# A GFNet mixing block followed by a SiLU feed-forward network: how the start of the kernel and its first 24 steps are arranged

## The chip, the core and the metric

The kernel runs on one core of a Trainium2 chip, in one launch. The metric is the device time of a run in microseconds. Five engines work beside each other: TensorE (PE; its weight loads are PEld), VectorE (DVE), ScalarE (ACT), GpSimd (POOL) and SyncE (SP). Each works through its own queue in the order in which the program issued its instructions[...].

## The reference

The input is `x` of 8 x 3008 x 256. It is filtered in the frequency domain along its second axis, and the result goes through a feed-forward network (FFN) row by row:

```python
X = np.fft.rfft(x, axis=1)
Y = X * (filt_r + 1j * filt_i)[None]
y = np.fft.irfft(Y, n=3008, axis=1).reshape(24064, 256)
h = y @ w_in                        # 256 x 2048
g = h * (1.0 / (1.0 + np.exp(-h)))
out = g @ w_out                     # 2048 x 256
```

The two weight matrices arrive in 64-bit floating point; the kernel rounds them to 32 bits on the chip.

## The kernel before

**The spectral part.** The Fourier transform of 3008 points is done as matrix products of 94 and 64 points, one batch at a time, in six groups `g`. `forward(g)` (L438) makes the second forward product on TensorE, `multiply(g, k)` (L454) multiplies it by the two filter parts on VectorE out of PSUM, `add(g, k)` combines the four products to a complex number, `inverse` goes back, `rows` evicts and writes to a DRAM tensor `d2`, `load_t4` reads `d2` back in another order, and `stage3` (L549) makes `y`, in two halves of each batch.

**The ramp.** Batch 0 cannot hide behind an FFN, since there is none yet. From L1028 on the program writes its order out by hand: `stage1_first` and 16 transposes, then per group `forward`, `multiply`, `inverse_first` (L495), `rows_first` (L515). For groups 0 and 1 GpSimd adds the products (`by_gpsimd`, L1010). For groups 2 to 5 nobody adds them: `inverse_first` runs twice as many matmuls and lets PSUM add. `load_t4` reads `d2` in three portions of rows (0 to 24, 24 to 32, 32 to 48), eight transfers each, some of them on the ACT queue. The four `stage3` calls that follow make the first half of `y`; then FFN step 0 can start.

**The FFN.** The tokens are cut in 48 pairs of blocks of n tokens (256, 256 and 240 in each half of a batch). Each pair needs 8 steps, one for each index `jp` of 256 hidden columns, 384 steps in all. A pair of blocks is multiplied by Strassen's method with 7 products instead of 8, so `tokens(pair)` (L709) first makes 4 differences on VectorE. A step runs two generators against each other: `hidden(step)` (L719) makes 7 products and the SiLU, and `project(step - 1)` (L778) makes 7 products of the step before, which add up over the 8 steps in four PSUM banks `acc` 0 to 3. `drain(pair, i)` (L803) copies a bank out after the eighth step; GpSimd then makes 7 sums, and `output` (L840) transposes and stores.

**Rounds.** Each step has 8 rounds (0 to 7). In a round each generator goes one product further, then `until` emits all pieces that are due. The hidden products of rounds 0 to 7 are: A11 into bank `px`; A12 into `pyz[:, 1]`, then VectorE makes g0 from it; S2 into `px`; S1 into `pyz[:, 0]`; S3 into `px`, then VectorE makes g2; nothing; A22 into `px`; S4 into `pyz[:, 0]`, then VectorE makes g1 from it. `px` and `pyz` have one buffer each. P0 to P6 below are the products of `project` in their order. `put(step, rnd, piece)` (L593) sets when a piece of spectral work or of weight work is emitted; a piece of a round comes after that round's products on every queue.

**Opened steps.** For 20 steps in the list `opened` (two for batch 1, three for each later batch) the program emits P0, P1 and some spectral products ahead of round 0. So `project` is two ahead and is held back in two rounds (L1154):

```python
held = work[1:] if step in opened and rnd in (0, 2) else []
work = [w for w in work if w in held or next(w, work) is not work]
```

**The weights.** 16 blocks `j` of weights are loaded raw (`load_weights`, L880), split into exponent and mantissa (`split_weights`, L907: two VectorE instructions, L920 and L923, and two on ACT), rounded (`round_weights`, L933: three on VectorE, L936, L938, L942), multiplied together into `w_t` (`place_weights`, L945: two, L951), and for each two blocks combined (`combine_weights`, L961: four). Blocks 0 to 8 are done before the FFN. Blocks 9 to 15 are done in steps 0 to 6:

```python
for j in range(9, NJ):
    put(j - 9, 1, lambda j=j: (split(j), rounded(j)))
    put(j - 9, 5, placed, j)
```

Their combining is put at round 5 mostly. Steps 0 to 7 also hold the `stage1` of batch 1, four matmuls in round 3 (L333, tile `pa`).

Of the kernel before, what the change touches and what calls it, by code (L numbers as in the profile page):

```python
# [167 lines left out]
def kernel(  # L168
# [98 lines left out]
    def spectral(b):  # L267
# [12 lines left out]
        def load_first():  # L280
# [10 lines left out]
            return view  # L291
# [162 lines left out]
        def multiply(g, k):  # L454
            if b == 0 and g == NG - 1:

                room = raws["first"].bitcast(FP32).rearrange("p (k i r c) -> p k i r c", k=2, i=2, r=2)
                z, pt = room[:, k, 0], room[:, k, 1]
            else:
                z = zpool.tile([128, 2, C], FP32, name=f"z_{b}_{g}_{k}", tag="z")  # L460
            if b == 0 and g == NG - 1:
                pass
            elif b == 0 and k == 1:
                pt = abcpool.tile([128, 3, C], FP32, name=f"p_{b}_{g}_{k}", tag="abc")[:, 0:2]
            else:
                pt = ppool.tile([128, 2, C], FP32, name=f"p_{b}_{g}_{k}", tag="p")
# [6 lines left out]
        def add(g, k):  # L473
            z, pt = prods[g][k]
            eng = nc.vector if b > 0 else nc.gpsimd
# [19 lines left out]
        def inverse_first(g):  # L495
# [3 lines left out]
            pairs = prods.pop(g)  # L499
            halves[g] = ps  # L500
            for h in range(2):
                table = e_t[:, g] if h == 0 else minus[g // 4][:, g % 4]
                terms = [(table[:, :, 0], 0, 0), (table[:, :, 1], 0, 1)]
                if g not in by_gpsimd:
                    terms += [(table[:, :, 1], 1, 0), (neg[h][:, g], 1, 1)]
                for t, (lhs, which, ri) in enumerate(terms):
                    for i in range(2):
                        rows = slice(64 * i, 64 * i + 64)
                        for k in range(2):

                            nc.tensor.matmul(out=ps[i][64 * k:64 * k + 64, h, :], lhsT=lhs[rows, k],
                                             rhs=pairs[k][which][rows, ri, :], start=(h == 0 and t == 0),
                                             stop=(t == len(terms) - 1), skip_group_check=True)

        def rows_first(g):  # L515
            for i, pool, tag in ((0, qpool, "q"), (1, opool, "o")):
                qt = pool.tile([128, 2, C], FP32, name=f"q_{b}_{g}_{i}", tag=tag)
                nc.scalar.copy(out=qt, in_=halves[g][i])
                a0 = 8 * g + 4 * i
                queue = nc.gpsimd if g == NG - 2 else nc.scalar  # L520
                queue.dma_start(out=d2[a0:a0 + 4].rearrange("a n h c -> (a n) h c"), in_=qt)
# [17 lines left out]
        def load_t4(g, first=0, last=2 * NS):  # L539
            if first == 0 and b == 0 and g in (2, 3):  # L540
                t4s[g] = tpool.tile([128, 4, C], FP32, name=f"t4_{b}_{g}", tag="t")
            elif first == 0:
                t4s[g] = t4pool.tile([128, 4, C], FP32, name=f"t4_{b}_{g}", tag="t4")
            for h in range(2):
                queue = nc.scalar if first == 32 and h == 1 else nc.sync
                queue.dma_start(out=t4s[g][64 * h + first:64 * h + last],
                                in_=d2[first:last, 4 * g:4 * g + 4, h, :])
# [30 lines left out]
        def evict_y(g, h):  # L578
# [7 lines left out]
                    load_t2=load_t2, forward=forward, multiply=multiply, add=add, inverse=inverse, inverse_first=inverse_first, rows_first=rows_first, even=even, rows=rows, load_t4=load_t4, stage3=stage3)  # L586
# [114 lines left out]

    def combine(eng, out, in0, in1, op):
        eng.tensor_tensor(out=out, in0=in0, in1=in1, op=op)  # L703
# [5 lines left out]
    def tokens(pair):  # L709

        n, yt = pairs[pair][3], channels(pair)
        t = typool.tile([128, 4, CH], FP32, name=f"ty_{pair}", tag="ty")
# [4 lines left out]
        ty[pair] = t  # L717

    def hidden(step):  # L719

        pair, jp = divmod(step, NJP)
        n, yt, t = pairs[pair][3], channels(pair), ty[pair]
# [55 lines left out]
    def project(step):  # L778

        pair, jp = divmod(step, NJP)  # L780
        n, g = pairs[pair][3], g_t.pop(step)
        if jp == 0:
            acc[pair] = {}
        last = jp == NJP - 1

        order = PROJECT
        if jp == 0 and step in joined:
            order = PROJECT[0:2] + PROJECT[3:5] + PROJECT[2:3] + PROJECT[5:]
        elif jp == 0:
            order = PROJECT[2:3] + PROJECT[0:2] + PROJECT[3:]  # L790
        for c, k, i, h in order:
            if i not in acc[pair]:
                acc[pair][i] = accps.tile([128, 2, 256], FP32, name=f"acc_{pair}_{i}", tag=f"a{i}")

            nc.tensor.matmul(out=acc[pair][i][:, h, 0:n], lhsT=w_t[:, jp, c, 1], rhs=g[:, k, 0:n],  # L795
                             start=(jp == 0 and h == 0), stop=last, skip_group_check=True)
            if last and (h == 1 or i == 3):
                drain(pair, i)
# [4 lines left out]
    def drain(pair, i):  # L803
        n = pairs[pair][3]

        if i == 0:
            results[pair] = spool.tile([128, 8, CH], FP32, name=f"s_{pair}", tag="s")
            if n < CH:
                gp.memset(results[pair][:, :, n:CH], 0.0)
        s = results[pair]  # L810
        if pair == len(pairs) - 1:
            return drain_last(pair, i, n, s, acc[pair])
        copy = v.tensor_copy if i % 2 else nc.scalar.copy
        if i < 3:
            copy(out=s[:, 2 * i:2 * i + 2, 0:n], in_=acc[pair][i][:, :, 0:n])  # L815
            return
        copy(out=s[:, 6, 0:n], in_=acc.pop(pair)[3][:, 0, 0:n])
        for o, a, b in ((2, 0, 2), (5, 0, 5), (3, 5, 3), (6, 3, 6), (0, 5, 1), (4, 0, 4), (1, 3, 1)):
            combine(gp, s[:, o, 0:n], s[:, a, 0:n], s[:, b, 0:n], ALU.add)

    def drain_last(pair, i, n, s, sums):

        def add(o, a, b):
            combine(v, s[:, o, 0:n], s[:, a, 0:n], b, ALU.add)
        if i == 0:
            nc.scalar.copy(out=s[:, 0:2, 0:n], in_=sums[0][:, :, 0:n])
# [361 lines left out]
```

## Time and profile before

| what | value |
|---|---|
| time, median of 3 runs | 2586.41 us (2585.56 to 2587.24) |
| the profiled execution, its time / its span | 2588.03 us / 2586.3 us |
| mean granted TensorE clock | 0.995 |
| busy: PE, PEld, DVE, ACT, POOL | 99%, 85%, 65%, 43%, 16% |
| PE busy in the first 100 us | 85.67 us |
| first matmul of FFN step 0 | 82.36 us |

The page gives shares over the whole span. The ramp is 3% of it, so anything that happens there has to be read from the timeline and the chain of waits for the first 100 us. From 82 us on, the profile can be read step by step: each step begins with a matmul into `px` from `y`. A plain step lasts 6.04 us with n = 256 and 5.67 us with n = 240; one with `stage1` in it mostly 7.84 to 7.97 us.

### The profile page before, as it was taken

The page shows a single profiled execution, that of the slowest core. Times are in us where ns is not written, and L with a number is a line of the kernel's source. Part 1 is how long each engine was busy: PE and PEld are TensorE (multiplying, and loading weights), DVE is VectorE, ACT ScalarE, POOL GpSimd, SP SyncE. Part 2 cuts the span into 40 slices and gives each one's busy share as a digit, 9 for nine tenths or more (in the row PEclk, how much of TensorE's full clock was granted, in tenths as well). Part 3 has the DMA queues.
Part 4 walks back from the last instruction along what each step waited for, and adds up shares of the span by engine and source line. Part 5 has one row for each costly group of instructions (what it writes and reads, how often), then busy time and mean ns, then how long its engine had stood idle before and what let it go on. Part 6 is the DMA issues. An engine that isn't in the chain of part 4 may idle for free.

```text
span 2586.3 us, 48366 instructions
## 1 busy us (share of the span) xinstructions
PE 2560.6 (99%) x18972; PEld 2198.1 (85%) x18972; DVE 1681.0 (65%) x3569; ACT 1113.9 (43%) x3014; POOL 424.9 (16%) x672
## 2 busy tenths in 40 slices
PE   8999999999999999999999999999999999999998
PEld 6688888888888888888888888888888888888987
DVE  7766666666666766666666666666666676555554
ACT  3544444444444444444444444444444444444443
POOL 2211211121112111211122111211121112101101
PEclk9899999999999999999999999999999999999999
DMA  8431232212222222231223222331232211210000
GB/s 276 142 90 45 68 83 67 60 53 82 63 63 64 71 65 58 70 78 59 68 51 89 58 66 58 79 76 52 64 74 67 73 45 27 65 20 16 9 17 17
DMA packets 200077, 171.08 MB, mean 66 GB/s; under 512 B 122116, under 2 KB 174196, under 8 KB 199060
## 3 DMA queue, kind: packets, MB, share of 16 engines
q1 hardware_dynamic: 178520, 117.04, 19.0%
q0 software_dynamic: 16928, 44.65, 5.4%
q10 hardware_dynamic: 4400, 6.29, 0.8%
q8 instruction: 149, 2.44, 0.4%
q14 instruction: 80, 0.66, 0.1%
HBM read 96.05 MB, written 81.26 MB: 69 GB/s over the span
## 4 chain that ended last, share of the span: by engine, by line
PE 95%; DVE 2%; DMA 1%; ACT 1%; issue 0%; ACTq 0%; SPq 0%; DVEq 0%
PE acc L795 43%; PE px L732 25%; PE pyz L732 19%; PE pd L560 3%; PE pb L446 2%; PE pc L489 2%; PE pf L416 1%; DMA w_t<-in_x_dram 0%; DVE g L703 0%; PE pa L342 0%; DMA filt<-in_filt_r_dram 0%; DMA d_t<-d_tbl 0%; PE pa L333 0%; DMA raw<-in_moe_w_out_dram 0%; ACT t L349 0%
## 5 line engine op out<-in xcount | busy, mean ns | idle before, releaser
L795 PE MATMUL acc<-g,w_t 128*128 128x256 f32 (+1 forms) x5376 | 1508.7, 375 | 0.4 <-DVE g L703 0.4
L795 PEld LDWEIGHTS acc<-g,w_t 128*128 128x128 f32 x5376 | 1021.3, 190 | 115.6 <-DVE g L703 0.8
L703 DVE TENSOR_TENSOR g<-pyz,abc 128x256 f32<-128x256 f32 (+1 forms) x1152 | 479.7, 416 | 614.9 <-ACT abc L753 360.1
L703 DVE TENSOR_TENSOR g<-g 128x256 f32<-128x256 f32 (+3 forms) x1152 | 599.3, 520 | 196.9 <-ACT g L736 183.7
L732 PE MATMUL px<-ty,w_t 128*128 128x256 f32 (+1 forms) x2304 | 678.1, 376 | 0.5 <-ACT abc L753 0.5
L736 ACT ACTIVATE g<-g 128x256 f32<-128x256 f32 (+1 forms) x1152 | 472.9, 410 | 250.1 <-DVE g L703 250.1
L703 POOL TENSOR_TENSOR s<-s 128x256 f32<-128x256 f32 (+1 forms) x329 | 255.1, 793 | 1412.7 <-DVE s L815 1307.6
L732 PEld LDWEIGHTS px<-ty,w_t 128*128 128x128 f32 x2304 | 432.3, 190 | 64.5 <-issue 8.2
L732 PE MATMUL pyz<-y,w_t 128*128 128x256 f32 (+1 forms) x1536 | 454.2, 377 | 0.0
L732 PEld LDWEIGHTS pyz<-y,w_t 128*128 128x128 f32 x1536 | 283.4, 189 | 48.3 <-DVE g L703 8.6
L747 ACT COPY abc<-px 128x256 f32<-128x256 f32 (+1 forms) x384 | 141.5, 368 | 364.6 <-PE px L732 364.6
L753 ACT COPY abc<-px 128x256 f32<-128x256 f32 (+1 forms) x384 | 141.9, 370 | 336.1 <-PE px L732 335.3
L736 ACT ACTIVATE g<-px 128x256 f32<-128x256 f32 (+1 forms) x384 | 146.1, 381 | 297.3 <-PE px L732 297.2
L732 PE MATMUL px<-y,w_t 128*128 128x256 f32 (+1 forms) x768 | 232.2, 384 | 2.0 <-ACT y L246 1.0
L732 PE MATMUL pyz<-ty,w_t 128*128 128x256 f32 (+1 forms) x768 | 225.7, 376 | 0.2 <-DVE g L703 0.2
L732 PEld LDWEIGHTS px<-y,w_t 128*128 128x128 f32 x768 | 140.3, 189 | 34.9 <-DVE y L582 5.8
L732 PEld LDWEIGHTS pyz<-ty,w_t 128*128 128x128 f32 x768 | 144.5, 190 | 18.8 <-DVE g L703 1.0
L740 ACT COPY abc<-px 128x256 f32<-128x256 f32 (+1 forms) x384 | 135.8, 354 | 45.0 <-PE px L732 45.0
L560 PEld LDWEIGHTS pd<-wi_t,t 48*64 48x64 f32 x4096 | 67.2, 138 | 30.9 <-ACT g L736 16.4
L560 PE MATMUL pd<-wi_t,t 48*64 48x47 f32 x4096 | 73.5, 236 | 5.7 <-issue 3.5
L428 POOL DMA_DIRECT2D d<-tf x144 | 71.7, 505 | 31.3 <-DVE tf L424 27.3
L815 ACT COPY s<-acc 128x512 f32<-128x512 f32 (+1 forms) x94 | 54.3, 578 | 47.5 <-PE acc L795 47.4
(118 smaller groups left out, 1312.7 us busy)
## 6 DMA issues: line engine op xcount, KB each, us to landing
t<-d SPq DMA_DIRECT2D x120, 192.0 KB
d<-q POOLq DMA_DIRECT2D x86, 256.0 KB, 2.6
t<-d SPq DMA_DIRECT2D x84, 256.0 KB
out_dram<-o SPq DMA_DIRECT2D x636, 32.0 KB
d<-tf POOLq DMA_DIRECT2D x144, 96.0 KB, 3.5
xr<-in_x_dram SPq DMA_DIRECT2D x6, 1472.0 KB
x_all<-in_x_dram SPq DMA_DIRECT2D x72, 96.0 KB
x_all<-xr SPq DMA_DIRECT2D x72, 96.0 KB
```

What stands on the lines that cost most here:

```text
L428: nc.gpsimd.dma_start(out=d1[k // 2, :, k % 2, n0:n0 + 4], in_=us["tf"][32 * k:32 * k + NS].rearrange("p q n c -> p (q n) c"))
L446: nc.tensor.matmul(out=ps[k][32 * j:32 * j + 32, ri, :], lhsT=d_t[rows, 4 * g + at, ri, :], rhs=t2[rows, at, :], start=True, stop=True)
L489: nc.tensor.matmul(out=ps[j][64 * k:64 * k + 64, a, :], lhsT=e_t[rows, g + a, k, ri, :], rhs=zs[k][rows, ri, :], start=(a == 0 and ri == 0 ...
L560: nc.tensor.matmul(out=ps[h][c0:c0 + 64, cb, i, :], lhsT=t4s[g][rows, i, 128 * cb + c0:128 * cb + c0 + 64], rhs=wi_t[rows, :], start=True, ...
L703: eng.tensor_tensor(out=out, in0=in0, in1=in1, op=op)
L732: nc.tensor.matmul(out=out, lhsT=w_t[:, jp, c, 0], rhs=rhs, start=start, stop=True, skip_group_check=True)
L736: nc.scalar.activation(out=g[:, k, 0:n], in_=g[:, k, 0:n] if src is None else src, func=AFT.Silu)
L740: nc.scalar.copy(out=sums[:, 0, 0:n], in_=xo)
L747: nc.scalar.copy(out=sums[:, 1, 0:n], in_=xo)
L753: nc.scalar.copy(out=sums[:, 2, 0:n], in_=xo)
L795: nc.tensor.matmul(out=acc[pair][i][:, h, 0:n], lhsT=w_t[:, jp, c, 1], rhs=g[:, k, 0:n], start=(jp == 0 and h == 0), stop=last, skip_group ...
L815: copy(out=s[:, 2 * i:2 * i + 2, 0:n], in_=acc[pair][i][:, :, 0:n])
```

## The change

**Ramp.** `load_t4` for the first half of `y` is replaced by `load_t4_first`: one area of 16 KB per partition, read by six transfers on SP (rows 0 to 16, 16 to 32, 32 to 48, two each). GpSimd adds the products of all groups, with VectorE taking the second of groups 4 and 5; `inverse_first` has 32 matmul instructions for every group. The first four `forward` calls are issued together. The last eviction of `rows_first` goes to VectorE. ACT's first filter loads wait for the last piece of `x` and no longer for the second. Blocks 0 to 3 of the weights are done before the FFN, instead of 0 to 8.

**FFN.** The first three pairs are cut in two runs each: `jp` 0-1 of pair 0, 0-3 of pairs 1 and 2, then the rest of each. The first run is copied out of PSUM, the second is added to it by VectorE. So the later weights are needed later, blocks 4 to 15 are done in steps 0 to 10 and 12, and their VectorE work is spread over more rounds. `tokens` runs six times for these pairs. The rounds in which an opened step holds `project` back are 1 and 2 instead of 0 and 2.

```diff
+        def load_t4_first(first, last):
+            for g in range(4):
+                t4s[g] = us["t4"][:, 4 * g:4 * g + 4]
+            for h in range(2):
+                nc.sync.dma_start(out=us["t4"][64 * h + first:64 * h + last], in_=d2[first:last, 0:16, h, :])
...
         def add(g, k):
             z, pt = prods[g][k]
-            eng = nc.vector if b > 0 else nc.gpsimd
+            eng = nc.vector if b > 0 or (g > 3 and k == 1) else nc.gpsimd
...
-                terms = [(table[:, :, 0], 0, 0), (table[:, :, 1], 0, 1)]
-                if g not in by_gpsimd:
-                    terms += [(table[:, :, 1], 1, 0), (neg[h][:, g], 1, 1)]
-                for t, (lhs, which, ri) in enumerate(terms):
+                for ri in range(2):
...
+                copy = nc.vector.tensor_copy if (g, i) == (NG - 1, 1) else nc.scalar.copy
+                copy(out=qt, in_=halves[g][i])
...
+    runs = [(0, 0, 2), (1, 0, 4), (2, 0, 4), (0, 2, 8), (1, 4, 8), (2, 4, 8)]
+    runs += [(pair, 0, NJP) for pair in range(3, len(pairs))]
...
+        if begin > 0:
+            combine(v, dst, dst, src, ALU.add)
+        else:
+            copy = v.tensor_copy if i % 2 else nc.scalar.copy
+            copy(out=dst, in_=src)
...
+    def round_weights(j, k):
...
+        if k == 0:
...
             v.tensor_scalar(out=e, in0=hi, scalar1=20, scalar2=0x7ff,
                             op0=ALU.logical_shift_right, op1=ALU.bitwise_and)
+            v.tensor_scalar(out=m, in0=hi, scalar1=0xfffff, scalar2=None, op0=ALU.bitwise_and)
+        elif k == 1:
             nc.scalar.activation(out=ef, in_=e, func=AFT.Relu, bias=bias_t[:, 0:1])
...
+        elif k == 2:
             v.scalar_tensor_tensor(out=mf, in0=lo, scalar=2.0 ** -52, in1=mf, op0=ALU.mult, op1=ALU.add)
-            if j not in (0, 2, 4, 6):
+            if not by_scalar:
                 v.tensor_scalar(out=e, in0=ef, scalar1=255.0, scalar2=float(1 << 23),
                                 op0=ALU.min, op1=ALU.mult)
-        for j in js[::-1]:
-            lo, hi, e, m, ef, mf = raws[j]
+        else:
             v.scalar_tensor_tensor(out=e, in0=hi, scalar=0x80000000, in1=e,
                                    op0=ALU.bitwise_and, op1=ALU.bitwise_or)
...
+    for g in range(4):
         part["forward"](g)
     for g in range(NG):
         for k in range(2):
             part["multiply"](g, k)
+            part["add"](g, k)
+        if g == 3:
+            part["forward"](5)
+        if g > 0:
+            inverse(g - 1)
+        if g == 1:
             part["forward"](4)
+    part["load_t4_first"](0, 16)
+    part["load_t4_first"](16, 32)
+    inverse(NG - 1)
+    part["load_t4_first"](32, 48)
+    second["load_x"](0)
+    weights(4, 5)
+    second["load_x"](1)
     combine_weights(0)
+    for k in range(4):
+        for j in (2, 3):
+            round_weights(j, k)
+    placed(2, 3)
+    combine_weights(1, eng=gp)
+    weights(6, 7)
+    idle(26)
     for g in range(4):
         part["stage3"](g)
-    weights(11, 12, 13)
+    weights(8, 9)
...
-    for j in range(9, NJ):
-        put(j - 9, 1, lambda j=j: (split(j), rounded(j)))
-        put(j - 9, 5, placed, j)
+    for j in range(4, NJ):
+        at = j - 4 if j < 15 else 12
+        for k, rnd in enumerate((1, 2, 4, 5)):
+            put(at, rnd, round_weights, j, k)
+        put(at, 6, placed, j)
         if j % 2:
...
+            for k, rnd in ((0, 3), (1, 5)):
+                put(at + 1, rnd, combine_weights, j // 2, k)
...
+    joined.update((2, 6, 10, 20))
...
+    begun = ((-2, 1), (0, 5), (4, 5), (8, 5), (14, 5), (18, 5))
+    early_stores = (((22, 1), (22, 5)), ((23, 1), (23, 5)), ((26, 1), (26, 4)))
...
-            held = work[1:] if step in opened and rnd in (0, 2) else []
+            held = work[1:] if step in opened and rnd in (1, 2) else []
```

## The prediction

> **What bounds the kernel now.** I read the page first. TensorE is busy for nearly the whole span, and 95% of the chain of waits is TensorE too. Busy time is no measure of lost time here, so I listed the start of each FFN step from the timeline. Over the whole kernel a plain step lasts 6.04 us (n = 256) or 5.67 us (n = 240), which is 14 products of 0.432 or 0.405 us. TensorE thus runs without gaps, and whatever makes it wait in a step is added to the end in full. Only the ramp has open time. Its last part, in the chain of waits of the first 100 us:
>
> ```profile
> 70.13 2.66 DMA t<-d
> 72.79 0.09 issue
> 72.88 5.59 PE pd L560 x246
> 78.47 2.45 issue
> 80.92 0.53 PE pd L560 x8
> ...
> 82.36 1.19 PE px L732 x2
> ```
>
> The FFN starts 9.48 us after `stage3` does; 2.45 us of that are waited for nothing visible. The second view is the timeline of FFN step 3 (start us, us, engine, line, tiles). It shows how much room VectorE has before TensorE notices:
>
> ```profile
> 111.56 0.69 DVE L936 SCALAR_TENSOR_TENSOR m<-raw,m 128x512 f32<-128x512 uint32 x1 [0.97 <-ACT m L924]
> 112.11 0.60 PE L732 MATMUL px<-ty,w_t 128*128 128x256 f32 x2
> 112.17 0.42 DVE L938 TENSOR_SCALAR e<-e 128x512 uint32<-128x512 f32 x1
> 112.62 0.69 DVE L942 SCALAR_TENSOR_TENSOR e<-raw,e 128x512 uint32<-128x512 uint32 x1
> 113.37 0.42 DVE L703 TENSOR_TENSOR g<-pyz,abc 128x256 f32<-128x256 f32 x1
> 113.71 0.87 DVE L703 TENSOR_TENSOR w_t<-w_t 128x256 f32<-128x256 f32 x2
> 114.50 0.75 DVE L951 TENSOR_TENSOR w_t<-m,e 128x256 f32<-128x256 f32 x2
> 115.17 0.42 DVE L703 TENSOR_TENSOR g<-pyz,abc 128x256 f32<-128x256 f32 x1
> 115.64 0.30 PEld L732 LDWEIGHTS pyz<-y,w_t 128*128 128x128 f32 x2 [0.23 <-DVE g L703]
> ```
>
> The line at 113.37 is g2 (round 4), that at 115.17 is g1 (round 7). Between them VectorE does the pieces of rounds 4 to 7: two combines, two placings, 113.71 to 115.17 = 1.46 us. The next step's A12 then has to wait for g1, since it writes the same one-buffer `pyz`: its weight load was held 0.23 us, and its product still started on the beat (115.65 = 114.79 + 2 x 0.43). So 1.46 us between g2 and g1 is just free; I count every us beyond it as lost. The rounding (L936 to L942) costs nothing in this step, because it stands in round 1, ahead of g2, beside the four `stage1` matmuls that start at 110.39.
>
> The third view is the timeline of an opened step:
>
> ```profile
> 437.17 0.59 PE L732 MATMUL pyz<-y,w_t 128*128 128x256 f32 x2
> 437.37 0.37 ACT L740 COPY abc<-px 128x256 f32<-128x256 f32 x1 [0.89 <-PE px L732]
> 437.61 0.59 PE L795 MATMUL acc<-g,w_t 128*128 128x256 f32 x2
> 437.88 0.42 DVE L703 TENSOR_TENSOR g<-pyz,abc 128x256 f32<-128x256 f32 x1 [1.24 <-PE pyz L732]
> 438.35 0.31 PEld L732 LDWEIGHTS pyz<-ty,w_t 128*128 128x128 f32 x2
> 438.47 0.59 PE L732 MATMUL pyz<-ty,w_t 128*128 128x256 f32 x2
> ```
>
> A12 runs at 437.17, then P2, S2 (at 438.04), S1. S1's weight load starts 0.05 us after g0 ends (438.30), on the beat with nothing to spare.
>
> [...] S1 writes the other half of `pyz` and still waits for VectorE's read. [...] The trace shows L923 at 0.95 us while GpSimd combines weights (64.48), and at 0.42 alone. [...] Here it was 0.50 from about 75 to 88 us, after 1.9 us of idling at 71 and with the small `stage3` matmuls.
>
> **The ramp.** Up to the first `multiply` nothing on the path changes: VectorE's 16 transposes (19.05 to 33.11) follow the arrival of `x`. ACT's first filters are issued some 3 us later (wait for the piece landing at 18.5, not 15.4); they have until about 39 us, when group 2 is multiplied, and land some 2 us sooner. If `x` alone has the queues, it may land up to 0.7 us sooner. I count zero.
> - VectorE: `multiply` of a group is 4 x 0.60 = 2.4 us from 34.83. GpSimd: `add` is 4 x 0.69 = 2.75 us per group from 36.27, so it is the slower; groups 0 to 3 end at 47.3. Group 4 and 5 are halved. VectorE's four adds cost 0.35 each alone and up to 0.9 beside GpSimd. The last sum ends at about 51.5 (50.9 to 52.7).
> - `inverse_first` is then 1.9 us: 53.5. Before, the last one ended at 62.9.
> - Eviction 0.6, two issues on ACT with their gaps: 54.9. Before, 64.93.
> - Landing in `d2`: a write issued at 51.24 to 51.56 released SP at 54.52, that is 2.95 us: 57.9. Then two issues of 0.4 us each and landing. Before, the last portion (eight transfers, 512 KB) took from 69.10 to 72.79, 3.7 us, some of it issue; two transfers of the same bytes: 3.4. `stage3` starts at 61.3 (60 to 63), not 72.88.
> - From there to the FFN 9.48 us as before. The weight transfers that fill the queues at 73 to 80 us now follow the last `t4` at once, so I keep the 2.45 us; `idle(26)`, 5.9 us from 53.6, ends 1.8 us before `stage3`, as it did, so I keep the slow clock too.
>
> FFN start 70.8 instead of 82.36: **-11.6 us** (-15 to -8). Blocks 2 and 3 (VectorE until 63.5, GpSimd until 67.5) are ready before step 1 needs them.
>
> **Steps 0 to 13.** Blocks 4 to 15 now stand with rounding in rounds 4 and 5 and placing in round 6. These are on VectorE's queue behind g2 and ahead of g1: L936 0.61, L938 0.45, L942 0.69, placing 0.67, together 2.42 us. Other pieces between g2 and g1, from the same rows: combining of round 5 0.79 (even steps from 2 on), `tokens` 1.52 (146.08 to 147.60; steps 0, 4, 8), two copies of `drain` 0.96 (steps 2, 6, 10), `multiply` 1.2 (step 12). Less the free 1.46 us:
> - steps 1, 3, 5, 7, 9: 0.96 each, 4.8
> - steps 2, 6, 10: 2.42 + 0.79 + 0.96 - 1.46 = 2.71 each, 8.1
> - steps 4, 8: 2.42 + 0.79 + 1.52 - 1.46 = 3.27 each, 6.5
> - step 0: 2.48; step 12: 2.16
>
> Sum 24.1. The kernel before loses some 1.5 us in these steps (7.84 to 7.97 against 7.77 of pure products, and 8.65 in step 6), which its better spread would recover: **+22.6 us** (12 to 30). What is gained in rounds 1 to 3, where VectorE then idles (it no longer waits 0.97 us for ACT), can't be used by an in-order queue.
>
> **Later steps.** `tokens` meets adds or transposes in rounds 4 to 6 of steps 14, 22 and 26 (0.7 + 1.52 - 1.46 = 0.75 each), and the added drains meet an add in step 20 (0.8): **+2.5** (0 to 4). No matmul is added by the runs; a boundary between pairs (step 8, 6.12 us) costs 0.1.
>
> **Opened steps.** Holding rounds 1 and 2 emits A11, P2, A12, S2, S1 where it was A11, A12, P2, S2, S1. A12 is one product (0.43) later, S1 is not; g0 follows A12, and S1 waits for g0. ACT's copy allows 0.05, so TensorE waits about 0.37 us, in 20 steps 7.4. In the seven opened at step 38 of a batch the next step already waits about 0.3 us for late evictions; that I take as absorbed: **+5.3** (0 to 8).
>
> **Sum.** -11.6 + 22.6 + 2.5 + 5.3 = +18.8. The profiled execution took 2588.03 us for a span of 2586.3; the median is 2586.41, to which I add: **2605 us**.
>
> **Rivals.**
> - *Lateness is absorbed* (faster). If TensorE waits only where VectorE's whole work in a step exceeds the step, only two steps stall. A step's own VectorE work is 2.5, rounding and placing 2.9, combining 1.4. Step 8: with `tokens` 8.3 against 5.7; step 10: with copies and one eviction of `y` 8.6 against 6.9 (5.9 + 1.0 of `stage3`). That is 4.3, less the 1.5 of before; later steps and holding cost nothing: -11.6 + 2.8, 2578 us. For it: TensorE ran on through steps whose VectorE work with its waits came to 7.7 of 7.85 us. Against: the 0.23 us wait above. It decides, other terms being nil, once steps 0 to 13 lose under 11.6 + 1.5 = 13 us.
> - *Half absorbed*: steps 0 to 13 cost 10, the rest 2: 2587 us, no change.
> - *The ramp gains little*: the transfers of `d2` queue behind each other[...]; -4 instead of -11.6: 2613 us. Before, a write issued at 57.63 released SP only at 63.31.
>
> **Numbers.** Forecast 0.61, absorbed 0.16, half absorbed 0.10, small ramp 0.13. The likeliest case alone reaches from 2596 to 2615; with the others the range is 2580 to 2618. About 0.2% (5 us) can be told from no change. Faster 0.15, same 0.08, slower 0.77.
>
> **What would show it.** Right: `stage3` at about 61 us, FFN at 71; in steps 1 and 3 the load of A12 waits 1 us for g1, with L936, L938, L942 behind g2; steps 4 and 8 longest; S1 in opened steps 0.3 to 0.4 us late. Wrong: steps 0 to 7 still at 7.9 us, or an FFN start above 78.

## The result, and the profile after

The changed kernel takes **2632.22 us** (median of four runs, 2628.96 to 2633.19) against 2586.74 for the kernel before beside it: ratio **1.0174**, 95% interval 1.0159 to 1.0189, so some 45 us slower. The forecast was 2605 us, from 2580 to 2618: the direction is right, the size is not. The profiled execution is the shortest of the four, 2628.96 us for a span of 2627.0; against the profiled execution before (span 2586.3) it is 40.7 us longer. From the starts of the FFN steps, read from both timelines:

| stretch, us | before | after | difference | forecast |
|---|---|---|---|---|
| up to FFN step 0 | 82.36 | 82.87 | +0.5 | -11.6 |
| steps 0 to 13 | 106.0 | 133.6 | +27.6 | +22.6 |
| steps 14 to 37 | 158.4 | 164.6 | +6.1 | +2.5 |
| steps 38 to 383 | 2221.7 | 2228.2 | +6.5 | +5.3 |

The ramp is where it went wrong. The chain of waits of the changed kernel (start us, us, what):

```profile
49.45 0.59 ACT q L516
...
50.07 5.42 DMA d<-q
...
55.57 0.59 ACT q L516
...
56.19 1.94 DMA d<-q
58.13 0.67 DVE q L516
58.80 0.03 DVE w_t L706
58.83 6.04 DMA d<-q
...
64.95 4.58 DMA w_t<-d
69.53 0.09 issue
69.62 0.41 PE pd L559 x2
70.04 1.58 issue
71.62 4.30 PE pd L559 x152
75.92 2.96 issue
78.88 3.08 PE pd L559 x102
...
82.87 1.19 PE px L737 x2
```

(`t4` is read into an area that the trace names `w_t`.) The inverse sums ended on time, at about 54.1. But writes of `d2` now take 5.4 and 6.0 us to land. They hold the two `q` and two `o` buffers that long, so the evictions of groups 4 and 5 wait for them (55.57, 58.13), the last write goes out at 58.83, and `t4` is whole at 69.5. `stage3` then has two gaps in which nothing visible is waited for.

The FFN's first step into the second, from the timeline (start, us, engine, line, tiles):

```profile
90.43 0.42 DVE L706 TENSOR_TENSOR g<-pyz,abc 128x256 f32<-128x256 f32 x1 [4.32 <-ACT abc L758]
...
90.77 0.68 DVE L961 SCALAR_TENSOR_TENSOR m<-raw,m 128x512 f32<-128x512 uint32 x1
...
91.37 0.42 DVE L963 TENSOR_SCALAR e<-e 128x512 uint32<-128x512 f32 x1
...
91.71 0.69 DVE L706 TENSOR_TENSOR ty<-y 128x512 f32<-128x512 f32 x1
...
92.43 0.89 DVE L706 TENSOR_TENSOR ty<-y,ty 128x256 f32<-128x256 f32 x2
93.23 0.68 DVE L966 SCALAR_TENSOR_TENSOR e<-raw,e 128x512 uint32<-128x512 uint32 x1
93.95 0.76 DVE L975 TENSOR_TENSOR w_t<-m,e 128x256 f32<-128x256 f32 x2
94.63 0.42 DVE L706 TENSOR_TENSOR g<-pyz,abc 128x256 f32<-128x256 f32 x1
...
95.10 0.81 PE L737 MATMUL pyz<-y,w_t 128*128 128x256 f32 x2 [2.35 <-DVE g L706]
...
95.70 1.06 PE L801 MATMUL acc<-g,w_t 128*128 128x256 f32 x2
...
96.56 1.06 PE L737 MATMUL px<-ty,w_t 128*128 128x256 f32 x2
```

Between g2 (90.43) and g1 (94.63) VectorE works 3.86 us, and A12 of step 1 waits 2.35 us for g1: the stall that was forecast. Two things were not seen. A product after the wait (two matmuls) takes 1.06 us where 0.59 is usual: half clock, which the windows view confirms (a granted clock of 0.50 from 96 to 99 us). And ahead of g2 VectorE idles 4.32 us, while TensorE does the four `stage1` products; e6 and e7 below move pieces there.

### The profile page after: what moved, and what is told of

It reads as the page before. It is cut to its first block, busy times and chain, and to the rows that moved or that the text cites. A ratio compares the mean times of both kernels' runs of the same rounds, so it can differ in the third digit from the quotient of the medians.

```text
span 2627.0 us, 48093 instructions
## 1 busy us (share of the span) xinstructions
PE 2565.1 (98%) x18812; PEld 2193.9 (84%) x18812; DVE 1698.2 (65%) x3609; ACT 1109.2 (42%) x3007; POOL 420.1 (16%) x670
## 4 chain that ended last, share of the span: by engine, by line
PE 92%; DVE 4%; DMA 2%; ACT 1%; issue 1%; ACTq 0%; DVEq 0%; SPq 0%
PE acc L801 42%; PE px L737 24%; PE pyz L737 19%; PE pd L559 3%; PE pb L447 2%; PE pc L489 2%; DVE g L706 1%; PE pf L417 1%; DMA x_all<-in_x_dram 1%; DMA d<-q 1%; PE pa L334 0%; PE pa L343 0%; DVE w_t L975 0%; DVE ty L706 0%; DVE e L966 0%
## 5 line engine op out<-in xcount | busy, mean ns | idle before, releaser
L706 POOL TENSOR_TENSOR s<-s 128x256 f32<-128x256 f32 (+1 forms) x315 | 243.0, 783 | 1433.1 <-DVE s L837 1305.2
L559 PEld LDWEIGHTS pd<-wi_t,t 48*64 48x64 f32 x3840 | 61.3, 135 | 25.5 <-ACT g L741 16.4
L870 DVE STREAM_TRANSPOSE o<-s 128x256 f32<-128x256 f32 x184 | 70.9, 423 | 0.8 <-issue 0.7
```

The source lines that it names most:

```text
L559: nc.tensor.matmul(out=ps[h][c0:c0 + 64, cb, i, :], lhsT=t4s[g][rows, i, 128 * cb + c0:128 * cb + c0 + 64], rhs=wi_t[rows, :], start=True, ...
L870: v.transpose(out=o[:, :, h, :], in_=result(pair, FINAL[2 * chunk + h], True))
```

## The experiments

Medians in us, each with that of the kernel before in the same comparison and the ratio to it:

| run | time | before | ratio (95%) |
|---|---|---|---|
| changed kernel | 2632.22 | 2586.74 | 1.0174 (1.0159-1.0189) |
| e1_loads_late | 2631.77 | 2586.84 | 1.0172 (1.0157-1.0188) |
| e2_reads_last | 2629.94 | 2586.84 | 1.0159 (1.0142-1.0176) |
| e3_buffers | 2629.97 | 2586.84 | 1.0164 (1.0149-1.0179) |
| e4_hold | 2623.26 | 2586.84 | 1.0137 (1.0122-1.0152) |
| e5_reads_held | 2634.85 | 2586.99 | 1.0183 (1.0168-1.0198) |
| e6_tokens | 2623.13 | 2586.99 | 1.0142 (1.0125-1.0159) |
| e7_rounds | 2619.85 | 2586.99 | 1.0126 (1.0111-1.0141) |
| e8_filler | 2644.08 | 2586.99 | 1.0222 (1.0206-1.0237) |
| e9_reads_split | 2621.45 | 2585.55 | 1.0136 (1.0121-1.0151) |
| e10_two_queues | 2633.39 | 2585.55 | 1.0183 (1.0166-1.0200) |
| e11_steps | 2607.46 | 2585.55 | 1.0083 (1.0068-1.0098) |
| e12_one_side | 2628.26 | 2586.08 | 1.0163 (1.0147-1.0178) |
| e13_wide_reads | 2630.65 | 2585.92 | 1.0174 (1.0153-1.0194) |
| c1_all | 2602.88 | 2586.08 | 1.0063 (1.0049-1.0076) |
| c2_all_late | 2605.80 | 2585.92 | 1.0078 (1.0061-1.0095) |
| b1_loads_late | 2584.37 | 2585.55 | 0.9993 (0.9985-1.0002) |
| b2_longer_idle | 2582.89 | 2586.08 | 0.9987 (0.9980-0.9993) |

The arrival of the filters moves the ramp by up to 3.5 us from one execution to the next, so ramps are compared from the first eviction of the inverse sums to the start of `stage3`: 29.98 us in the changed kernel (39.64 to 69.62), and 30.1 to 32.4 in the seven runs that leave this part as it is (e1, e2, e4, e6, e7, e8, e11).

### The ramp: what makes the writes of d2 late

**e2**, all reads of `t4` called after the last inverse sums:

```diff
-    part["load_t4_first"](0, 16)
-    part["load_t4_first"](16, 32)
     inverse(NG - 1)
+    part["load_t4_first"](0, 16)
+    part["load_t4_first"](16, 32)
     part["load_t4_first"](32, 48)
```

> The changed kernel, with all six transfers of t4 issued after the last write of d2, none early. Reads in the way of the writes: the writes of groups 3 to 5 land in 2.5 to 3.5 us instead of 5 to 6, the evictions of groups 4 and 5 wait under 1 us for their buffers, and the last write lands at 57 to 59.5 us instead of 64.9. The whole of t4 (1.5 MB) must then be read behind it, 5 to 8 us, so that stage 3 starts at 63 to 67 us instead of 69.6; total -3 to -6 us. Rival, the writes are slow by themselves: they still take 5 to 6 us, the last lands at 64 to 65, stage 3 starts at 70 to 73, total 0 to +4 us.

The first read was still issued early, at 49.49 us: moving the call past work of other engines changed nothing in SP's own queue. So this is the changed kernel once more, and the expectation was not tested; its 2.3 us less show the scatter.

**e3**, four areas of their own for the evictions of groups 4 and 5:

```diff
+                if g == 4:
+                    if i == 0:
+                        us["room4"] = upool.tile([128, 2, 2, C], FP32, name="room4", tag="u")
+                    qt = us["room4"][:, i]
+                elif g == 5:
+                    qt = tpool.tile([128, 2, 2, C], FP32, name=f"q_{b}_{g}_{i}", tag="t")[:, 0]
```

> The changed kernel, with the evictions of groups 4 and 5 in four areas of their own instead of the two q and two o buffers, so that they wait for no older write. Buffers alone: the evictions of group 5 end at 55 to 56 us instead of 58.8, the writes issue at once, and the last lands at 58 to 60; stage 3 starts at 63 to 65 instead of 69.6, total -5 to -7 us. Rival, the transfers are the limit (early reads and writes share the engines): evictions end early but the last write still lands at 62 to 65 us, stage 3 starts at 67 to 70, total 0 to -2.5 us.

The rival holds. The waits for buffers are gone, but the writes still land in 4.0 to 4.3 us, and then the last portion of `t4` takes 6.3: first eviction to `stage3` 29.3 us instead of 30.0 to 32.4.

**e5**, the last portion first on SP's queue, so that all reads stand behind the last write:

```diff
-    part["load_t4_first"](0, 16)
-    part["load_t4_first"](16, 32)
     inverse(NG - 1)
     part["load_t4_first"](32, 48)
+    part["load_t4_first"](0, 16)
+    part["load_t4_first"](16, 32)
```

> The changed kernel, with the transfers of rows 32 to 48 of t4 put first on SP's queue, so that all six reads of d2 stand behind the last write (moving the calls behind the last inverse sums left SP's order as it was). Reads in the way of writes: the writes of groups 3 to 5 land in 2.5 to 4 us (5.4 and 6.0 before), the evictions of groups 4 and 5 wait under 1.5 us for a buffer, the last write lands at 58 to 61 us instead of 65, then the 1.5 MB of reads take 6.5 to 9 us: stage 3 starts at 65.5 to 69 instead of 69.6, total 0 to -4 us. Rival, the writes are limited by themselves: the last lands at 63 to 65 all the same and stage 3 starts at 70.5 to 74, total +1 to +5.

Its chain of waits:

```profile
52.26 0.59 ACT q L516
52.87 2.86 DMA d<-q
...
61.42 12.84 DMA w_t<-d
...
74.35 4.30 PE pd L559 x151
```

and the queues of its transfers from 61 to 66 us (packets, MB, share of 16 engines):

```profile
q1 hardware_dynamic: 630, 0.61, 112.5%
```

Half of it as expected: without reads beside them the writes land in 2.86 us, as before the change, no eviction waits over 0.6 us for a buffer, and the last is done at 56.5 (forecast 54.9 with its issue). So the early reads hold up the writes. But the reads themselves, expected in 6.5 to 9 us, take 12.8 from the issue of the last of them and 15.2 from that of the first, at 59.08: SP's queue moves 0.61 MB in 5 us, 120 GB/s, with all engines full, 143 ns for a packet of 1 KB (112.5% x 16 x 5 us / 630). In the kernel before the same queue needed 52 ns (496 packets, 53.7% of 55 to 58 us).

**e9**, each read cut into four, with the halves of the partitions taking turns. The theory behind it, an assumption of the author's, was that the number of partitions a transfer goes to limits its rate (120 GB/s in e5, with 16 partitions a transfer; 165 GB/s from 55 to 58 us in the kernel before, with 24), and that turns between two ranges of partitions lift that limit.

```diff
-            for h in range(2):
-                nc.sync.dma_start(out=us["t4"][64 * h + first:64 * h + last], in_=d2[first:last, 0:16, h, :])
+            for g in range(4):
+                for h in range(2):
+                    nc.sync.dma_start(out=t4s[g][64 * h + first:64 * h + last],
+                                      in_=d2[first:last, 4 * g:4 * g + 4, h, :])
```

> The changed kernel, with each read of t4 cut into four of 64 KB (four channels rows of 1 KB for 16 partitions), the two halves of the partitions taking turns on the one queue, as the kernel before cut them; the rows read and when stay the same. [...] Then packets of these reads take 50 to 100 ns, the writes of groups 4 and 5 land in 3 to 4.5 us, the last at 60 to 63 us, stage 3 starts at 64 to 67.5 instead of 69.6: total -2 to -5.5 us. Rival, 1 KB pieces of d2 are slow whatever they go to, or the turns are too coarse on one queue: 120 to 145 ns as before, and 24 issues of 0.4 us more: total 0 to +3.

The chain of waits; SP's issues of the reads; and the queues from 60 to 64 us (q10 is ACT's, q1 SP's):

```profile
58.23 3.48 DMA d<-q
...
63.60 2.49 DMA w_t<-d
66.10 0.14 issue
66.23 7.38 PE pd L561 x256
...
73.63 0.80 ACT y L246
...
74.52 1.19 PE px L739 x2
```

```profile
60.60 6.71 SPq L526 DMA_DIRECT2D w_t<-d  x13
```

```profile
q10 hardware_dynamic: 380, 0.68, 44.5%
q1 hardware_dynamic: 530, 0.44, 40.6%
```

A packet of the reads takes 49 ns, and first eviction to `stage3` 24.5 us. The FFN starts at 74.5 instead of 82.9, although the first eviction came 2.1 us later, and the total falls by some 10 us, double what was expected. Not all of it is the form of the reads:

- Up to `stage3` two things come together. The write in the chain lands in 3.5 us instead of 6.0, so that the last portion begins to be issued 21.9 us after the first eviction instead of 25.3. And `stage3` starts 2.6 us behind that issue instead of 4.7: its first call needs only two of the portion's eight transfers, for the issues above run until 67.3 us and `stage3` starts at 66.23.
- The other 5 us are the gaps in `stage3`, which are gone in this run. c1 below has the same reads and has the gaps: 24.1 us up to `stage3`, and 13.0 from there to the FFN, where e9 has 8.3 and the changed kernel 13.25.

So **the form of the six reads cost some 5.5 of the 12 us by which the ramp fell short**; that it makes the gaps too is not shown.

Packets of 49 ns instead of 143 don't mean that the split reads move more bytes. Shares above 100% (112.5% above, 103.0% below) say that packets overlap on an engine, so that a packet's time holds waiting as well. With no write beside them, the last portion of the changed kernel (66 to 68 us) and that of e9 (63.5 to 67 us) show

```profile
q1 hardware_dynamic: 338, 0.33, 103.0%
q1 hardware_dynamic: 628, 0.51, 58.6%
```

which is 165 and 146 GB/s. The large reads fill the engines, the split ones leave them four tenths of the time. Writes beside the large reads landed in 5.4 and 6.0 us, beside small ones in 3.4 to 4.4 (e9, and e12 below). Whether the partitions that a transfer goes to are behind it, and not its size, three runs were to tell. e10 keeps the large reads and gives the two halves of the partitions two queues; that this raises their rate was assumed.

> The changed kernel, with the reads of t4 for partitions 64 and up issued by GpSimd instead of SP, so that both halves run side by side; sizes and rows as they were. [...] the last portion lands in 3 to 3.6 us instead of 4.6, the writes of groups 4 and 5 in 3.5 to 5, stage 3 starts at 64 to 67: total -2.5 to -5.5 us. Rival, the reads are slow by their 1 KB pieces: 120 GB/s, stage 3 at 69 to 71, total -0.5 to +1.5.

```diff
-                nc.sync.dma_start(out=us["t4"][64 * h + first:64 * h + last], in_=d2[first:last, 0:16, h, :])
+                queue = nc.gpsimd if h else nc.sync
+                queue.dma_start(out=us["t4"][64 * h + first:64 * h + last], in_=d2[first:last, 0:16, h, :])
```

No gain: first eviction to `stage3` 31.1 us, last portion in 7.8. But the halves didn't run side by side. GpSimd issued its last read at 68.01; from 68 to 71 us, while SP's was read, its queue (q0) has no packet, and from 71 to 74 us it has

```profile
q0 software_dynamic: 69, 0.26, 58.1%
```

So this run says nothing on reads of both halves at once.

> As the run with split reads (24 transfers of 64 KB on one queue), with only the order changed: four times partitions 0 to 15 and then four times 64 to 79 of each portion, where that run took turns. If a run of transfers to the same 16 partitions is what is slow[...]: packets take 80 to 130 ns against 47 to 55 with turns, stage 3 starts at 67.5 to 71 instead of 66.2, total within 4 us of the changed kernel (2628 to 2633). If the size of a transfer is (256 KB in 16 KB rows against 64 KB in 4 KB rows): 47 to 60 ns, stage 3 at 65 to 67, total as with turns (2619 to 2624).

```diff
-            for g in range(4):
-                for h in range(2):
+            for h in range(2):
+                for g in range(4):
```

Small transfers without turns: 48 to 54 ns a packet beside the writes and 69 after them (62 to 66 us, 628 packets, 67.3%), where e9 has 52; 25.5 us to `stage3`. So it is the size more than the order, though the order is not nothing. The total, only 4 us under the changed kernel's, is that of the other case, since gaps of 1.81 and 1.67 us stood in `stage3` again.

**e13**, the large reads to 48 partitions each instead of 16, behind the last write. The expectation has two cases: first, that the number of partitions limits a large read, which was an assumption; second, that its row of 16 KB does.

> The changed kernel with all of t4 read behind the last write as in the run with held reads, but by two transfers to 48 partitions each (768 KB, still 16 KB for a partition) instead of six to 16. There the 1.5 MB took 12.8 us at 120 GB/s and 144 ns for each packet. [...] 65 to 80 ns, 1.5 MB in 7 to 8.5 us, stage 3 from 67 to 69. If it is the long row of 16 KB by itself: 120 to 145 ns and 11.5 to 13.5 us, stage 3 from 71.5 to 74.5. The total follows: -1 to -3 us, or +1 to +4, against the changed kernel.

```diff
-    part["load_t4_first"](0, 16)
-    part["load_t4_first"](16, 32)
     inverse(NG - 1)
-    part["load_t4_first"](32, 48)
+    part["load_t4_first"](0, 48)
```

Two transfers to 48 partitions: `t4` in 13.1 us, and from 64 to 68 us this line of the queues, which is 122 ns for a packet:

```profile
q1 hardware_dynamic: 591, 0.59, 112.7%
```

Three times the partitions bring 148 GB/s instead of 120: their number is at most a part of it. Shown is that large transfers, with rows of 16 KB for a partition in pieces of 1 KB, are read at some 120 to 165 GB/s with the engines full, and transfers with rows of 4 KB, issued 0.5 us apart, at 130 to 146 GB/s with the engines at 59 to 67%. Whether the long row does it or the backlog of large transfers stays open.

**e1**, the loads behind `t4` only after `stage3`'s last eviction, by a 4-byte transfer that reads its result:

```diff
-    second["load_x"](0)
-    weights(4, 5)
-    second["load_x"](1)
...
-    weights(6, 7)
     idle(26)
     for g in range(4):
         part["stage3"](g)
+    nc.sync.dma_start(out=warm[0:1, 0:1], in_=y[0, 0][0:1, 1, HALF - 1:HALF])
+    second["load_x"](0)
+    weights(4, 5)
+    second["load_x"](1)
+    weights(6, 7)
```

> The changed kernel, with the input tiles of the second sequence and weight blocks 4 to 7 issued only once the last eviction of the first inverse transform (L573) is done, by a 4-byte transfer that reads its result. Loads in the way: if these loads lengthen the last portion of t4 (4.58 us)[...], the portion lands in 3.0 to 3.6 us, the two issue gaps (1.58 and 2.96 us) shrink to 0 to 1 us, and stage 3 to the first step of the FFN takes 9 to 10.5 us instead of 13.25. The rounding of block 4 may then wait for its words in steps 0 and 1 (2 to 5 us lost again). Total -6 to +1 us. Rival, the gaps come from stage 3 itself: 13 us and both gaps stay, total 0 to +5.

`stage3` in its chain:

```profile
74.75 1.44 issue
76.19 7.12 PE pd L559 x254
```

The long gap is gone, the short one stays; from `stage3` to the FFN 9.9 us instead of 13.25. The portion of `t4` did not get faster (4.46 us), step 0 took 1.9 us more and step 1 as much less. The total is the same within its scatter.

### The steps

**e7**, rounding and placing ahead of g2:

```diff
-        for k, rnd in enumerate((1, 2, 4, 5)):
+        for k, rnd in enumerate((1, 1, 2, 3)):
...
-        put(at, 6, placed, j)
+        put(at, 3, placed, j)
```

> The changed kernel, with the four pieces of a weight block's rounding in rounds 1, 1, 2, 3 and its placing in round 3, instead of 1, 2, 4, 5 and 6: of VectorE's work between the evictions g2 and g1 only combinations and tokens are left. Theory (that stretch sets the loss, VectorE's idle 4.3 us ahead of g2 hide the rest): the 0.9 us of each odd step and most of the 2.1 to 3.3 us of the even ones go, the half clock behind them in steps 1, 3, 5 too: the first 14 steps together 18 to 26 us shorter, total -18 to -26 us. Rival, the pieces delay g2 as much as they delayed g1: total 0 to -5 us. Halfway, where no stage 1 of the second sequence gives cover (steps 8 to 12): -10 to -15.

Steps 0 to 13 lose 15.4 us instead of 27.6, total -12: the halfway case, so the pieces are not all free there. A12 of step 1 waits 0.23 us (VectorE's g1 and the product, from the timeline), and the clock stays full (granted 1.00 from 95.5 to 104.5 us):

```profile
96.35 0.42 DVE L706 TENSOR_TENSOR g<-pyz,abc 128x256 f32<-128x256 f32 x1
...
96.82 0.70 PE L737 MATMUL pyz<-y,w_t 128*128 128x256 f32 x2 [0.23 <-DVE g L706]
```

**e6**, tokens in round 3:

```diff
-    begun = ((-2, 1), (0, 5), (4, 5), (8, 5), (14, 5), (18, 5))
+    begun = ((-2, 1), (0, 3), (4, 3), (8, 3), (14, 3), (18, 3))
```

> The changed kernel, with the token combinations of the first runs (three instructions of VectorE, 1.45 us) in round 3 instead of 5, ahead of the eviction g2 and not between g2 and g1. In steps 0 and 4 VectorE is idle 4.3 us ahead of g2, so that they would be hidden there. Theory (only work between g2 and g1 is lost[...]): 1.45 us gone in each of steps 1 and 5, and with the wait cut from 2.35 to 0.9 us the half clock too (1.5 each): the two steps 12.2 to 9.2..10.7, that of the third (step 9) by up to 1.4; total -4 to -7 us. Rival, the time is VectorE's whole work: 0 to -1.

Step 1 falls from 12.17 to 9.08 us and step 5 from 12.19 to 9.32, 3 us each for 1.45 us of work: the wait of 2.35 us is 0.95, and no product behind it is slow (0.59 us each, granted clock 1.00). Total -8 to -9, a little over what was expected; 1.7 us of it are luck, since step 3, whose wait is the same, found its clock full here (10.21 us instead of 11.89).

**e8**, eight matmuls of no use before A12 in steps 1, 3 and 5. They share the bank of the running sum in `px`, whose result they change in these steps:

```diff
+        for _ in range(8 if step in (1, 3, 5) else 0):
+            nc.tensor.matmul(out=px[:, 256:384], lhsT=wx_t, rhs=wx_t, start=True, stop=True,
+                             skip_group_check=True)
         mm(zo, A12, yt[:, 1, 0:n], True)
```

> The changed kernel, with eight matmuls of no use (about 2.05 us by their own row) put on TensorE in steps 1, 3 and 5 where it waits 2.35 us for g1, into columns of the px bank that nothing reads. If that wait brings the clock down to half for the eight matmuls behind it: no clock under 0.9 there, steps 1, 3 and 5 1.2 to 1.7 us shorter each (12.2 to 10.6), total -3.5 to -5 us. Rival, the clock falls for another reason, or the wait alone makes the 4.2 us: 0, or up to +2 where the fillers overrun the wait.

Badly placed: writing `px`, they waited themselves for ACT's copy of it, 3.05 us in step 1, and ran behind the wait. The 12 us lost say nothing on whether fillers in the wait would help.

**e4**, the hold of the opened steps as before:

```diff
-            held = work[1:] if step in opened and rnd in (1, 2) else []
+            held = work[1:] if step in opened and rnd in (0, 2) else []
```

> The changed kernel, with the projections of the opened steps held back in rounds 0 and 2 again instead of 1 and 2. If the later hold is what lengthens these steps: each of the 20 opened steps 0.43 us shorter (step 52 from 5.71 to 5.28, step 86 from 5.88 to 5.45), total -8.6 us. If half is absorbed by the step behind it: -4. Rival, the opened steps are longer for another reason: 0.

As the theory has it: step 52 from 5.71 to 5.29, step 86 from 5.88 to 5.45; total -7 to -9.

**e11**, rounding in round 1 and placing in round 5, with e6 and e4:

```diff
-        for k, rnd in enumerate((1, 2, 4, 5)):
-            put(at, rnd, round_weights, j, k)
-        put(at, 6, placed, j)
+        for k in range(4):
+            put(at, 1, round_weights, j, k)
+        put(at, 5, placed, j)
```

> The changed kernel, with three things put back or moved in the FFN alone: the whole rounding of a block in round 1 and its placing in round 5 as in the kernel before, the tokens of the first runs in round 3, the hold of the opened steps in rounds 0 and 2. If these losses are separate they add up (-12 for the rounds, -9 for the tokens, -8.6 for the hold by single runs): -26 to -30, about 2604 us, and the first 14 steps together within 5 us of the kernel before. If rounds and tokens cure the same waits: -18 to -22. Rival, four more blocks in the FFN and split runs cost by their sheer number of instructions: not under -18, with 8 us or more left over the kernel before in the first 14 steps.

-24.8, between adding up and the same cure. Steps 0 to 13 still lose 13.4 us to the kernel before, where under 5 were expected, steps 14 to 37 6.0: this much of the third case holds.

### All together, and the kernel before

**c1** is e11 with the reads of e9 and more useless matmuls ahead of `stage3`; **c2** is c1 with the late loads of e1.

```diff
-    idle(26)
+    idle(38)
```

> The changed kernel with all that single runs showed undone at once: reads of t4 split and taking turns, rounding in round 1 and placing in round 5, tokens in round 3, hold in rounds 0 and 2; and 12 matmuls of no use more (3.1 us) ahead of stage 3, where TensorE waited 3.15 us and the clock was half from there to the first step. If the causes add up: 2607.5 - 10.8 = 2597 us, and if the clock holds through stage 3 (7.3 us to 3.7 to 5.5, first step 1 us shorter) 2592 to 2595. Rival, the clock falls all the same: 2596 to 2599. What stays over the kernel before is then that of more instructions in the FFN.

> The kernel with everything undone at once, and in addition the input tiles and weight blocks 4 to 7 issued only after the last eviction of the first inverse transform. There two issue gaps (1.52 and 3.70 us) stood in stage 3, with the loads beside it; in the changed kernel this move took the longer gap away, in the kernel before the only one. If the gaps come from these loads: stage 3 from 65.7 us in 4.0 to 7.5 us, first step at 71 to 74.5 instead of 78.7; at most 3 us given back in steps 0 and 1, where block 4 waits for its words: total -2 to -6 us against the run without it (2597 to 2601). Rival, gaps of another cause: 0 to +3 us.

c1 is 29 us under the changed kernel, but 8 to 11 over the forecast: `stage3` starts 24.1 us after the first eviction, as in e9, but its chain has gaps of 1.52 and 3.70 us. In c2 the long one is gone and the FFN starts at 74.3, but block 4 comes too late: step 0 takes 12.37 us, and 5 us are given back. What is left in c1 over the kernel before, 17 us, is, by its trace, -3.7 in the ramp, +14.6 in steps 0 to 13, +7.3 in steps 14 to 37 and -1.1 later. Three split runs and five more blocks in the FFN have that price in these forms; it was not split further.

**b1** is the kernel before with its loads behind `t4` moved as in e1; **b2** is b1 with `idle(44)` for `idle(34)`.

```diff
-    second["load_x"](1)
-    weights(10)
...
+    nc.sync.dma_start(out=warm[0:1, 0:1], in_=y[0, 0][0:1, 1, HALF - 1:HALF])
+    weights(10)
+    second["load_x"](1)
     weights(11, 12, 13)
```

> The kernel before, with the second input tile of the next sequence and weight blocks 10 to 13 issued only after the last eviction of the first inverse transform, by a 4-byte transfer that reads its result. With the changed kernel the same move took away the longer of its two issue gaps in stage 3. If the 2.45 us gap of the kernel before has the same cause: gap under 0.6 us, total -1 to -2.5 us (2584.3 to 2586), unless block 10 comes too late for its rounding in step 1 (+1 to +3 back). Rival: 0.

> The kernel before with the late loads of the last run, and 10 matmuls of no use more (44 for 34, 2.6 us) ahead of stage 3, where TensorE waited 2.0 us for t4 in two pieces and its clock fell to half for stage 3 (7.1 us) and the first step. If the wait is what drops the clock: stage 3 in 3.6 to 5.5 us, the first step 1 us shorter, at up to 1 us of delay: total -2.5 to -5 us against the kernel before (2581 to 2584), -1.5 to -4 against the run with late loads alone. Rival, stage 3's matmuls of 48 x 64 with 47 columns count as idle for the clock: half clock all the same, total 0 to +1 against late loads alone.

b1: the 2.45 us gap is gone, -1.2 us in the median, not told apart from none. TensorE in b2, from the timeline:

```profile
63.11 10.09 PE L1007 MATMUL idle<-wx_t 96*128 96x128 f32 x88
73.13 3.95 PE L560 MATMUL pd<-wi_t,t 48*64 48x47 f32 x228
77.91 0.67 PE L560 MATMUL pd<-wi_t,t 48*64 48x47 f32 x28 [0.83 <-issue]
79.68 1.19 PE L732 MATMUL px<-y,w_t 128*128 128x256 f32 x2 [1.10 <-DVE y L244]
```

No wait ahead of `stage3`, and its 256 products run at full clock (1.00 in the windows up to 78 us): 5.5 us from the first to the end of the last, gap included, where b1 needed 8.4 (70.85 to 79.28). **2582.89 us, ratio 0.9987 (0.9980 to 0.9993), is shorter than both kernels.** How much of it is the wait filled with useless matmuls is not told apart: from the first eviction to the FFN b2 takes 38.4 us and b1 40.0, but the intervals of their ratios overlap.

## Why the prediction was wrong

- **The ramp, the step that failed** (-11.6 forecast, +0.5 measured). Up to the end of the inverse sums it held, 54.1 for 53.5. The failing term is "Landing in `d2`: a write issued at 51.24 to 51.56 released SP at 54.52, that is 2.95 us", taken from a write with no large read beside it. The change puts large early reads beside the writes; the prediction put nothing down for what they do to the writes, nor for the buffers that a late write keeps. Eviction and issue of the last write came 3.3 us later than reckoned (buffers), its landing 3.1, the last portion ("two transfers of the same bytes: 3.4") 1.2, the sums 0.6, and `stage3` to FFN took 13.25 us for 9.48. (The 9.48 count from 72.88; from its first products, at 70.90, the kernel before has 11.46.) With the reads behind the writes (e5) a write lands in 2.86 us and no eviction waits over 0.6 us for a buffer; with the reads cut as before (e9) first eviction to `stage3` is 24.5 us instead of 30.0. The gaps in `stage3` stay without a cause. The rival "the transfers of `d2` queue behind each other" had the first half of the mechanism, with 0.13; it still gave the ramp -4, and nothing more to the steps.
- **Steps 0 to 13** (+22.6, measured +27.6). The mechanism was right: the sum gave step 8 3.27 and step 12 2.16 us, and the steps behind them, whose A12 waits, are 3.30 and 2.16 longer than before; e6 and e7 took such losses away. What the sum lacks is the clock. Steps 1, 3 and 5 took 4.3, 4.1 and 4.3 us more where 2.5 to 3.3 were reckoned, because behind each of these waits four products (eight matmuls) ran at half clock, 1.7 us a step (granted clock 0.50 for 3.41 us from 95.56, 116.04 and 136.52). The prediction saw VectorE idle ahead of g2 (4.32 us in step 0), and that its queue, worked through in order, can't use it; that the `tokens` of steps 0 and 4 could stand there (e6) was the cheap repair.
- **Later steps** (+2.5, measured +6.1): under-sized. Its own items add up to 3.1. Steps 15, 21, 23 and 27, behind those it named, took 4.2 us more; steps 16 to 20 and 24 took 2.0 more that it didn't name. Only e6, e11, c1 and c2 moved a piece here, the `tokens` of steps 14 and 18; steps 14 to 37 changed by 0.1 us in e6.
- **Opened steps** (+5.3, measured 0.43 in each of 20, 8.6): 0.37 was close (the trace marks S1's wait for g0 in each, 0.14 to 0.15 us of idle TensorE); that the seven at step 38 absorb it was wrong (5.46 to 5.89). One of the 20 is step 12. Of the other 8.2 us 6.5 remain in the table, because three steps that are not opened (88, 184, 208) took over 10 us in the trace before and 9.1 to 10.0 in the one after. So that the sum came near the forecast is luck.
- **VectorE beside GpSimd.** The 0.95 us that the prediction reads for L923 come again in the changed kernel: VectorE's add took 0.95 us at 48.18, beside an add of GpSimd's that took 0.91 instead of 0.72, and 0.41 at 52.10, after GpSimd's last. Neither trace marks a wait between the two engines there; why they are slower beside each other is not shown.
- **The rival "lateness is absorbed"**, the one on the other side, is refuted by the wait of 2.35 us at 95.10, and so is "half absorbed", with 10 us for steps 0 to 13 that cost 27.6.

## What to carry to other kernels

A transfer's cost is not its bytes alone: before merging many small reads into a few large ones, look up what else needs the same engines at that time, and in what form the reads leave room for it. Here the large reads moved their bytes about as fast (121 to 165 GB/s against 130 to 146), and the loss showed as late writes and then as missing buffers far from them. Ask of every piece on an in-order queue between which two deadlines it stands: in steps 0 and 4 the 1.45 us of `tokens` were free ahead of one eviction, and cost 3 us behind it. A call moved in the program past work of other engines moved nothing on its own queue (e2).

## What was not expected of the hardware

- A wait of about 2.2 us of TensorE was followed by half the clock in one execution and not in another: ahead of the same product in step 3 the changed kernel waited 2.18 us and ran the next product in 1.06 us, e4 waited 2.17 and ran it in 0.59. In the traces of both kernels all changes of the granted clock lie whole multiples of 3.413 us apart, in the changed kernel at 64.84, 88.74, 95.56, 98.98, 116.04, 119.46, 136.52, 139.94 and 2621.43 us. The changed kernel and e4, two stretches of that length each around the wait (length, TensorE busy, granted clock, DMA):

```profile
112.63:116.04 3.41, 1.23 (x6) 1.00 0.46 125
116.04:119.46 3.42, 3.42 (x9) 0.50 0.00 0
```

```profile
113.10:116.51 3.41, 1.58 (x8) 1.00 0.58 183
116.51:119.93 3.42, 3.08 (x13) 1.00 0.00 0
```

From step 1 to step 13 of the changed kernel, three stretches at full clock of which TensorE idled 2.18 to 2.35 us were each followed by one at half clock; none of which it idled 1.86 us or less was. Waits of 2.25, 2.99 and 2.31 us, which end at 157.39, 175.31 and 192.50, lie in two stretches each, and the clock stayed at 1.00. That it matters how a wait lies in these stretches is the author's reading; no run varied it. The step is 1.7 us longer for it (11.89 and 10.20), a part of the changed kernel's wider scatter.
- Small products of 48 x 64 kept the full clock in b2, where no wait stood ahead of them: granted 1.00 from 70 to 78 us, 228 in 3.95 us, 17 ns each. In e1 254 took 7.12 us and in e9 256 took 7.38, 28 and 29 ns each to the end. That is the pace of the changed kernel (152 in 4.30 us, 28 ns each), where the granted clock was 0.50 from 64.84 to 88.74 us. In the kernel before it was 0.50 from 74.57 to 88.22.
- The gaps in `stage3` have two sorts. The long one (2.45 to 3.70 us) came only with loads beside it, but not in every such run (not in e9 and e12); the short one (1.4 to 1.8 us) came without loads too (e1, c2). Their cause is not shown.
